# Gated products of an attention-and-GLU kernel: four pieces of 576 tokens, each as two halves of 288, in place of five pieces of up to 480

## The chip, the cores and the metric

The kernel runs on one core of one Trainium2 chip. The metric is the device time of one launch in microseconds (us); lower is better. The kernel before took 980.77 us (median of three runs, 980.37 to 981.58).

Five engines work side by side, each through its own queue in order: PE (TensorE; PEld is its weight load), DVE (VectorE), ACT (ScalarE), POOL (GpSimd) and SP (SyncE, which here issues every DMA). Engines wait for one another through semaphores.

## The reference

Queries are averaged in pairs (1152 to 576 rows per head), attention runs over 4 batches x 8 heads, and its result, 2304 tokens of 512 features, goes through a gated linear unit with a hidden width of 1536:

```python
q_pool = q.reshape(B, H, S // 2, 2, D).mean(axis=3)        # B=4, H=8, S=1152, D=64
scores = scale * np.matmul(q_pool, k.transpose(0, 1, 3, 2))
attn = softmax(scores)
x = np.matmul(attn, v)  ->  (2304, 512)
gate = 1.0 / (1.0 + np.exp(-(x @ w_gate)))                  # w_gate, w_val: 512 x 1536
out  = (gate * (x @ w_val)) @ w_out                         # w_out: 1536 x 512
```

## The kernel before, in words

Every float32 operand of a product is split into a high and a low fp32r part; a product of two operands is three matmuls (high x high, high x low, low x high).

**Attention.** Heads are taken one after the other (`attend`), each in two groups of 288 query columns (`GR`, `half`). Per head PE does the maxima's products (L354, 384 columns, reduced by DVE at L358), the scores (L438, two matmuls of 288), and the products with the values (L480 with the high part, L484 with the low part; in batch 0 L455). ACT takes the exponentials (L442, L470), DVE forms the low parts (L473), POOL sums the denominators (L502). Two heads make a pair; `normalise` divides the pair's result per group of 288 and writes the x tile's two parts: ACT the high (L594), POOL the low (L598).

**The gated part** (`gated`) runs per piece of tokens. A piece needs x of all four pairs of a batch. It has three thirds (`th`). A third makes four g tiles: each needs a gate and a value product of 12 matmuls over the piece's N tokens (`product`, L674), then tanh on ACT (L709), gate times value on DVE (L716), the split of g on ACT (L720) and POOL (L724). Then four output products (12 matmuls each, over the four g tiles), summed into `opart` by ACT (L749) or DVE (L751), and stored in the last third (L761). The weights are loaded by SP from a DRAM copy (L685): a wg tile (1 MB, gate and value) per g tile, a wo tile (0.5 MB) per output product; there are two wo slots. That DRAM copy is made by `convert` during the first batches: per tile two DVE instructions (L626, L631), three on ACT, one on POOL.

**Order.** The kernel hands every operation to a planner (`Plan`) with an engine, an assumed duration and a priority, and the planner writes out one fixed order per engine. `product` takes one of six PSUM banks (slot "b") and keeps it until ACT or DVE has read the result. The gated products of a piece get priorities spread over one batch's length, so that they lie between the attention of the next batch.

**Pieces.** `CUTS` (L167) divides the 2304 tokens at 480, 960, 1440 and 1920. A piece that crosses a batch's end waits for the next batch (L788 to 791), so one piece each follows batches 0, 1 and 2, and the last two pieces (480 and 384 tokens) follow batch 3, after all attention.

Of the kernel before, what the change touches and what calls it, by code (L numbers as in the profile page):

```python
# [158 lines left out]
def attention_glu_kernel(ctx: ExitStack, tc: tile.TileContext, qT, kT, vt_in, v, wg, wv, wo, out):  # L159
# [6 lines left out]
    CHUNK = 480  # L166
    CUTS = [min(k * CHUNK, B * SQ) for k in range(6)]  # L167
    NCH = len(CUTS) - 1

# [23 lines left out]
    LATE = {"x": 3, "wg": 1}  # L193
# [13 lines left out]
    def change_first():  # L207
# [13 lines left out]
    SHAPE = {"x": [128, 2, CHUNK], "wg": [128, 2, 2, 4, 128], "el": [128, GN], "acc": [128, GN],  # L221
# [25 lines left out]
        "g": tiles("g", [128, 2, CHUNK], F32R),  # L247
        "opart": tiles("opart", [128, CHUNK], F32),
# [4 lines left out]
        "sg": tiles("sg", [128, CHUNK], F32),  # L253
# [303 lines left out]
    def normalise(p, g, st):  # L557
# [23 lines left out]
        q = a  # L581
        while q < b:
            t = p // 4 * SQ + q
            c = max(k for k in range(NCH) if CUTS[k] <= t)
            o = t - CUTS[c]
            n = min(CUTS[c + 1] - t, b - q)
            key = (c, p % 4)
            first = key not in xs
            if first:
                xs[key] = (pl.hold("x"), [])  # L590
            xh, ops = xs[key]

            def hi(xh=xh, o=o, q=q, n=n):
                nc.scalar.activation(out=tl(xh)[:, 0, o:o + n], in_=tl(st["y"])[:, q:q + n], func=ACTF.Copy)  # L594

            def lo(xh=xh, o=o, q=q, n=n):
                x = tl(xh)
                nc.gpsimd.tensor_tensor(out=x[:, 1, o:o + n], in0=tl(st["y"])[:, q:q + n],  # L598
                                        in1=x[:, 0, o:o + n].bitcast(F32), op=ALU.subtract)

            f = pl.op("ACT", act(n), hi, s + 0.2, after=[nm], uses=[st["y"]] + ([] if first else [xh]),
                      take=[xh] if first else [])
            ops.append(pl.op("POOL", pool(n), lo, s + 0.2, after=[f], uses=[xh, st["y"]]))
            q += n

# [51 lines left out]
    def gated(ch, base, steps):  # L657
        base += 10
        step = steps / 36.0
        t0 = CUTS[ch]  # L660
        N = CUTS[ch + 1] - t0
        n_g = [0]
        acc = {}

        def product(at, parts, uses, after):
# [25 lines left out]
        for th in range(3):  # L691
            gs = {}
            for m_ in range(4 * th, 4 * th + 4):
                wh, lw = weights("wg", m_, base + step * n_g[0])
                sg, gh = pl.hold("sg"), pl.hold("g")
                for s in range(2):
                    at = base + step * n_g[0]
                    n_g[0] += 1

                    def parts(kc, wh=wh, s=s):  # L700
                        w, x = tl(wh), tl(xs[ch, kc][0])
                        return [(w[:, h, s, kc], x[:, l, 0:N]) for h, l in ((0, 0), (0, 1), (1, 0))]

                    ms, last = product(at, parts, lambda kc, wh=wh: [wh, xs[ch, kc][0]],
                                       lambda kc, lw=lw: [lw] + xs[ch, kc][1])
                    if s == 0:

                        def post(ms=ms, sg=sg):
# [22 lines left out]
            for dm in range(4):  # L731
# [3 lines left out]
                if th == 0:  # L735
                    acc[dm] = [pl.hold("opart"), None]
# [29 lines left out]
    xs = {}  # L766
# [80 lines left out]
```

## Time and profile before

| | us |
|---|---|
| median of three runs | 980.77 |
| the profiled execution | 980.11 |
| its span (all engines, first to last instruction) | 978.3 |
| PE / DVE / ACT / POOL busy | 935.5 / 697.7 / 636.0 / 682.1 |

The profile is one execution. Its page gives busy time by engine, a row of digits that shows each engine's busy share in 40 slices of 24.5 us, and the costliest groups of instructions with the mean duration of one. Matmuls overlap in PE's pipeline: one instruction is drawn some 300 to 380 ns long, though the next starts earlier. What a matmul costs is the distance between starts, and that is read from the timeline. "Idle before" an instruction is the time in which its engine did nothing, with the operation whose end released it.

### The profile page before, as it was taken

To read this page: it belongs to the slowest core of one execution; us is meant where nothing else is said; L and a number is where in the kernel's file an instruction comes from. 1 tells how busy PE (TensorE), PEld (TensorE's weight loads), DVE (VectorE), ACT (ScalarE), POOL (GpSimd) and SP (SyncE) were. 2 spreads that over 40 slices of the span, in tenths; PEclk is the share of its full clock that TensorE was granted. 3 is DMA by queue.
4 is the path that set the end of the run, shared out by engine and by line. 5 is a ranking of instruction groups with operands and counts; after the bars stand their busy time and mean duration, and the time that the engine had idled before them with its cause. 6 is when DMAs were issued, how large, how long until landed. Compare 5 with 4: busy or idle time off the path is not lost.

```text
span 978.3 us, 15851 instructions
## 1 busy us (share of the span) xinstructions
PE 935.5 (96%) x5136; PEld 837.3 (86%) x5136; DVE 697.7 (71%) x1386; ACT 636.0 (65%) x1605; POOL 682.1 (70%) x691
## 2 busy tenths in 40 slices
PE   6999999999879999999999999999999999999997
PEld 3878787988779888899889999998989888888996
DVE  6598888898988988887988898888988540111011
ACT  3779898978879668877776877777777632211211
POOL 7578797999998978888786887878877531211111
PEclk9999999999989999999999999999999999999999
DMA  7588887366876664345454455454342255656762
GB/s 169 150 263 257 274 267 232 118 216 201 258 263 198 214 216 144 102 136 156 133 154 140 134 157 154 137 163 147 105 131 87 86 187 198 215 189 242 255 248 86
DMA packets 54163, 175.62 MB, mean 180 GB/s; under 512 B 14656, under 2 KB 17216, under 8 KB 46400
## 3 DMA queue, kind: packets, MB, share of 16 engines
q1 hardware_dynamic: 54080, 174.61, 56.2%
q8 instruction: 40, 0.66, 0.3%
q14 instruction: 43, 0.35, 0.1%
HBM read 150.99 MB, written 23.59 MB: 178 GB/s over the span
## 4 chain that ended last, share of the span: by engine, by line
PE 77%; DVE 13%; ACT 5%; issue 2%; DMA 2%; POOL 1%; POOLq 0%; SPq 0%; ACTq 0%; DVEq 0%
PE bank L674 41%; PE bank L438 13%; PE bank L354 7%; PE bank L484 5%; PE bank L480 5%; PE bank L455 4%; DVE pm L358 3%; DVE cr L626 2%; DVE cr L631 2%; DMA wo<-wo_d 2%; DVE el L473 1%; DVE dh L545 1%; PE bank L487 1%; PE bank L549 1%; ACT eh L442 1%
## 5 line engine op out<-in xcount | busy, mean ns | idle before, releaser
L674 PE MATMUL bank<-x,wg 128*128 128x480 f32 (+1 forms) x1440 | 339.4, 373 | 0.9 <-ACT r L534 0.4
L358 DVE TENSOR_REDUCE pm<-bank 128x1 f32<-128x384 f32 x480 | 256.8, 549 | 46.0 <-PE bank L354 42.1
L674 PEld LDWEIGHTS bank<-x,wg 128*128 128x128 f32 x1440 | 259.5, 189 | 25.6 <-ACT r L534 1.6
L502 POOL TENSOR_TENSOR acc<-acc,eh 128x288 f32<-128x288 f32 x240 | 198.1, 825 | 59.4 <-ACT eh L442 48.6
L442 ACT ACTIVATE eh<-bank 128x288 fp32r<-128x288 f32 x432 | 176.6, 409 | 84.8 <-PE bank L438 79.6
L473 DVE TENSOR_TENSOR el<-bank,eh 128x288 fp32r<-128x288 f32 x432 | 192.2, 452 | 44.0 <-ACT bank L470 39.9
L354 PE MATMUL bank<-KA,QA 128*128 128x384 f32 x480 | 171.0, 372 | 12.1 <-ACT KA L336 7.9
L438 PE MATMUL bank<-QA,KA 128*128 128x288 f32 x576 | 173.4, 305 | 7.3 <-DVE sg L716 4.7
L470 ACT ACTIVATE bank<-bank 128x288 f32<-128x288 f32 x432 | 177.5, 411 | 0.0
L724 POOL TENSOR_TENSOR g<-sg,g 128x480 fp32r<-128x480 f32 (+1 forms) x60 | 71.3, 1189 | 143.3 <-ACT g L720 142.5
L674 PE MATMUL bank<-g,wo 128*128 128x480 f32 (+1 forms) x720 | 167.0, 371 | 4.3 <-DMA wo<-wo_d 2.1
L438 PE MATMUL bank<-QB,KB 128*128 128x288 f32 x576 | 169.3, 297 | 1.2 <-DVE QB L373 1.2
L674 PEld LDWEIGHTS bank<-g,wo 128*128 128x128 f32 x720 | 129.5, 188 | 19.0 <-DMA wo<-wo_d 3.1
L484 PE MATMUL bank<-el,vt 128*128 128x288 f32 x432 | 131.1, 304 | 7.0 <-DVE el L473 6.7
L480 PE MATMUL bank<-eh,vt 128*128 128x288 f32 x432 | 128.6, 298 | 2.1 <-ACT eh L442 2.1
L438 PEld LDWEIGHTS bank<-QA,KA 128*128 128x128 f32 x576 | 109.3, 190 | 16.7 <-DVE sg L716 5.0
L716 DVE SCALAR_TENSOR_TENSOR sg<-sg,bank 128x480 f32<-128x480 f32 (+1 forms) x60 | 37.8, 631 | 112.4 <-PE bank L674 111.6
L354 PEld LDWEIGHTS bank<-KA,QA 128*128 128x128 f32 x480 | 92.6, 194 | 28.5 <-DVE pm L358 13.9
L438 PEld LDWEIGHTS bank<-QB,KB 128*128 128x128 f32 x576 | 109.4, 190 | 3.3 <-DVE QB L373 1.7
L339 POOL TENSOR_TENSOR KB<-kr,KA 64x576 fp32r<-64x576 f32 x64 | 95.9, 1503 | 6.6 <-ACT KA L336 2.0
L484 PEld LDWEIGHTS bank<-el,vt 128*128 128x128 f32 x432 | 81.8, 189 | 16.8 <-DVE el L473 11.9
L720 ACT ACTIVATE g<-sg 128x480 fp32r<-128x480 f32 (+1 forms) x60 | 35.1, 585 | 88.8 <-DVE sg L716 67.7
(58 smaller groups left out, 1228.7 us busy)
## 6 DMA issues: line engine op xcount, KB each, us to landing
wg<-wg_d SPq DMA_DIRECT2D x60, 1024.0 KB, 4.9
wo<-wo_d SPq DMA_DIRECT2D x60, 512.0 KB, 3.7
kr<-in_kT_dram SPq DMA_DIRECT2D x64, 288.0 KB, 5.4
wg_d<-cs SPq DMA_DIRECT2D x24, 512.0 KB, 5.3
qr<-in_qT_dram SPq DMA_DIRECT2D x32, 288.0 KB, 4.3
vr<-in_v_dram SPq DMA_DIRECT2D x24, 288.0 KB, 4.2
cr<-in_wg_dram SPq DMA_DIRECT2D x12, 512.0 KB, 5.8
cr<-in_wv_dram SPq DMA_DIRECT2D x12, 512.0 KB, 4.8
```

Source lines behind the costliest of these rows:

```text
L339: nc.gpsimd.tensor_tensor(out=tl(kh)[1][HI, s], in0=tl(kr)[HI, s], in1=tl(kh)[0][HI, s].bitcast(F32), op=ALU.subtract)
L354: nc.tensor.matmul(out=tl(m)[:, 0:384], lhsT=tl(qh)[0][:, t * 128:(t + 1) * 128], rhs=tl(kh)[0][:, j * 384:(j + 1) * 384], start=True, sto ...
L358: nc.vector.tensor_reduce(out=tl(pm)[:, t, j:j + 1], in_=tl(m)[:, 0:384], axis=AXX, op=ALU.max)
L438: nc.tensor.matmul(out=tl(m)[:, 0:GN], lhsT=tl(hd["k"])[k][:, ks], rhs=tl(hd["q"])[k][:, a:b], start=(k == 0), stop=(k == 1))
L442: nc.scalar.activation(out=tl(eh), in_=tl(m)[:, 0:GN], func=ACTF.Exp, scale=1.0 / 16.0)
L470: nc.scalar.activation(out=p, in_=p, func=ACTF.Exp, scale=1.0 / 16.0)
L473: nc.vector.tensor_tensor(out=tl(el), in0=tl(m)[:, 0:GN], in1=tl(eh).bitcast(F32), op=ALU.subtract)
L480: nc.tensor.matmul(out=tl(av[0])[:, 0:GN], lhsT=pair(c, w), rhs=tl(eh), start=(c == 0), stop=(c == NC - 1))
L484: nc.tensor.matmul(out=tl(av[1])[:, 0:GN], lhsT=pair(c, 1 - w), rhs=tl(el), start=(c == 0), stop=(c == NC - 1 and not mine_c))
L502: nc.gpsimd.tensor_tensor(out=tl(acc), in0=tl(e0).bitcast(F32) if two else tl(acc), in1=tl(e1).bitcast(F32), op=ALU.add)
L674: nc.tensor.matmul(out=ps[:, 0:N], lhsT=l, rhs=r, start=(n == 0 and j == 0), stop=(n == 3 and j == 2))
L724: nc.gpsimd.tensor_tensor(out=g[:, 1, 0:N], in0=tl(sg)[:, 0:N], in1=g[:, 0, 0:N].bitcast(F32), op=ALU.subtract)
```

## The change

The pieces become the four batches, 576 tokens each. One weight tile brought in by DMA serves a whole piece, but no PSUM bank holds 576 float32 columns, so every product is made twice, for tokens 0 to 288 and 288 to 576 (`GR`), each half in a bank of its own with its own tanh, gate, split and output sum. The x tiles become 576 wide (8 in place of 12), the g and opart tiles 576 wide (4 each as before), the sg tiles 288 wide (4 in place of 2). `normalise` writes each group of 288 in one piece. Line numbers of the changed kernel: gated products L662, gate times value L706, weight loads L673, scores L434, value products L476 and L480, maxima L350 and L354, conversion L611 and L616.

```diff
-    CHUNK = 480
-    CUTS = [min(k * CHUNK, B * SQ) for k in range(6)]
-    NCH = len(CUTS) - 1
...
-        "y": 2, "r": 2, "tt": 1, "x": 12, "g": 4, "opart": 4, "wg": 3, "wo": 2, "cr": 3, "cs": 2, "sg": 2,
+        "y": 2, "r": 2, "tt": 1, "x": 8, "g": 4, "opart": 4, "wg": 3, "wo": 2, "cr": 3, "cs": 2, "sg": 4,
...
-    LATE = {"x": 3, "wg": 1}
+    LATE = {"x": 2, "wg": 1}
...
-        step = steps / 36.0
-        t0 = CUTS[ch]
-        N = CUTS[ch + 1] - t0
+        step = steps / 72.0
+        t0 = ch * SQ
...
-                        nc.tensor.matmul(out=ps[:, 0:N], lhsT=l, rhs=r, start=(n == 0 and j == 0), stop=(n == 3 and j == 2))
+                        nc.tensor.matmul(out=ps[:, 0:GN], lhsT=l, rhs=r, start=(n == 0 and j == 0), stop=(n == 3 and j == 2))
...
                 for s in range(2):
+                    for hf, (a, b) in enumerate(GR):
+                        at = now()
+                        if s == 0:
+                            sgs[hf] = [pl.hold("sg"), None]
+                        sg = sgs[hf][0]
+
+                        def parts(kc, wh=wh, s=s, a=a, b=b):
+                            w, x = tl(wh), tl(xs[4 * ch + kc, 0])
+                            return [(w[:, h, s, kc], x[:, l, a:b]) for h, l in ((0, 0), (0, 1), (1, 0))]
...
+            for dm in range(4):
+                wh, lw = weights("wo", 4 * th + dm, base + step * n_g[0])
...
+                for hf, (a, b) in enumerate(GR):
+                    at = now()
...
-        for ch in range(NCH):
-
-            if (CUTS[ch + 1] - 1) // SQ == b:
-                gated(ch, PB * (ch + 1), PB)
+        gated(b, PB * (b + 1), PB)
```

The planner writes a new order. Two places of it, before and after, follow. In the rows, `el`, `eh` are the parts of the exponentials, `vt` the values, `cr` the conversion's tile, `KA`/`QA`, `QB` the keys and queries; "waits" names the semaphore of the engine or DMA queue waited for.

The first place is in batch 1, some 285 us into the profiled execution, on DVE: two conversions follow each other. Before:

```order
L358 TENSOR_REDUCE pm_107<-bank 128x1 [waits PE_49]
L626 SCALAR_TENSOR_TENSOR cr_134<-cr_134 128x512 [waits DMAHW6_49]
L631 SCALAR_TENSOR_TENSOR cr_134<-cr_134 128x512 [waits DVE_49]
L626 SCALAR_TENSOR_TENSOR cr_135<-cr_135 128x512 [waits DMAHW3_49,Activation_49]
L631 SCALAR_TENSOR_TENSOR cr_135<-cr_135 128x512 [waits DVE_49]
L716 SCALAR_TENSOR_TENSOR sg_139<-sg_139,bank 128x480 [waits PE_49]
L473 TENSOR_TENSOR el_1426<-bank,eh_97 128x288 [waits Activation_49]
```

After:

```order
L354 TENSOR_REDUCE pm_107<-bank 128x1 [waits PE_49]
L611 SCALAR_TENSOR_TENSOR cr_131<-cr_131 128x512 [waits DMAHW6_49]
L616 SCALAR_TENSOR_TENSOR cr_131<-cr_131 128x512 [waits DVE_49]
L611 SCALAR_TENSOR_TENSOR cr_132<-cr_132 128x512 [waits DMAHW3_49]
L616 SCALAR_TENSOR_TENSOR cr_132<-cr_132 128x512 [waits DVE_49]
L706 SCALAR_TENSOR_TENSOR sg_136<-sg_136,bank 128x288 [waits PE_49]
L469 TENSOR_TENSOR el_1419<-bank,eh_97 128x288 [waits Activation_49]
```

Nothing moved on DVE: the four conversion instructions still stand together, with the gate product (now 288 wide) right behind them. PE at the same place, before:

```order
L484 MATMUL bank<-el_1425,vt_88 128x288 [waits DVE_49]
L438 MATMUL bank<-QA_79,KA_73 128x288
L438 MATMUL bank<-QB_82,KB_76 128x288
L480 MATMUL bank<-eh_97,vt_88 128x288 [waits Activation_49]
L354 MATMUL bank<-KA_74,QA_80 128x384 [waits DVE_49]
L438 MATMUL bank<-QA_79,KA_73 128x288 [waits DVE_49]
```

After:

```order
L480 MATMUL bank<-el_1418,vt_88 128x288 [waits DVE_49]
L434 MATMUL bank<-QA_79,KA_73 128x288
L434 MATMUL bank<-QB_82,KB_76 128x288
L350 MATMUL bank<-KA_74,QA_80 128x384 [waits DVE_49]
L476 MATMUL bank<-eh_97,vt_88 128x288 [waits Activation_49]
L662 MATMUL bank<-x_113,wg_127 128x288 [waits DVE_49]
```

In both the last row waits for DVE's gate product behind the conversions to give back its PSUM bank; a score's product stood there before, a gated product stands there now.

The second place is PE's end of the program: the last output products, over the four g tiles and alternating between the two wo slots. Before:

```order
L674 MATMUL bank<-g_122,wo_132 128x384 [waits DMAHW6_49]
L674 MATMUL bank<-g_122,wo_132 128x384 x2
L674 MATMUL bank<-g_123,wo_132 128x384 x3
L674 MATMUL bank<-g_124,wo_132 128x384 x3
L674 MATMUL bank<-g_125,wo_132 128x384 x3
L674 MATMUL bank<-g_122,wo_133 128x384 [waits DMAHW0_49,DVE_49]
```

After:

```order
L662 MATMUL bank<-g_119,wo_129 128x288 [waits DMAHW7_49,DVE_49]
L662 MATMUL bank<-g_119,wo_129 128x288 x2
L662 MATMUL bank<-g_120,wo_129 128x288 x3
L662 MATMUL bank<-g_121,wo_129 128x288 x3
L662 MATMUL bank<-g_122,wo_129 128x288 x3
L662 MATMUL bank<-g_119,wo_129 128x288 [waits DVE_49]
L662 MATMUL bank<-g_119,wo_129 128x288 x2
L662 MATMUL bank<-g_120,wo_129 128x288 x3
L662 MATMUL bank<-g_121,wo_129 128x288 x3
L662 MATMUL bank<-g_122,wo_129 128x288 x3
L662 MATMUL bank<-g_119,wo_130 128x288 [waits DMAHW2_49,DVE_49]
```

A wo tile now has 24 matmuls behind its one DMA wait, where it had 12. Over the whole program PE has 3456 gated matmuls of 288 columns where it had 1728 of 480 and 432 of 384. Behind the last attention matmul stand 909 gated matmuls of 288 now, and 453 of 480 and 432 of 384 before.

## Rows read from the trace of the kernel before

**Rows 1.** The page: span, busy time by engine, share, instructions.

```profile
span 978.3 us, 15851 instructions
PE 935.5 (96%) x5136; PEld 837.3 (86%) x5136; DVE 697.7 (71%) x1386; ACT 636.0 (65%) x1605; POOL 682.1 (70%) x691
```

**Rows 2.** Five stretches: length, busy by engine, granted clock, DMA share, GB/s.

```profile
240.00:300.00 60.00, 51.95 (x279) 47.12 (x280) 54.37 (x104) 49.49 (x120) 55.86 (x53) 0.91 0.73 237
300.00:400.00 100.00, 98.15 (x566) 88.60 (x565) 90.29 (x186) 75.32 (x199) 89.04 (x92) 1.00 0.54 180
400.00:794.00 394.00, 387.96 (x2274) 355.69 (x2273) 328.68 (x694) 290.11 (x773) 313.37 (x342) 1.00 0.44 136
...
0.00:794.00 794.00, 759.06 (x4252) 677.38 (x4253) 670.52 (x1340) 604.59 (x1547) 653.68 (x665) 0.99 0.56 174
794.00:978.30 184.30, 176.47 (x886) 159.94 (x884) 27.18 (x46) 31.44 (x58) 28.41 (x26) 1.00 0.59 205
```

**Rows 3.** PE's timeline, pieces of 480 and 384: start, length, line, operands, count.

```profile
829.92 5.37 PE L674 MATMUL bank<-g,wo 128*128 128x480 f32 x24
835.13 6.12 PE L674 MATMUL bank<-x,wg 128*128 128x480 f32 x27
...
940.37 4.38 PE L674 MATMUL bank<-g,wo 128*128 128x384 f32 x24
944.58 1.74 PE L674 MATMUL bank<-x,wg 128*128 128x384 f32 x9
```

**Rows 4.** The same view, first and last of two unbroken series of 288-column matmuls.

```profile
787.90 0.30 PE L484 MATMUL bank<-el,vt 128*128 128x288 f32 x1
...
789.10 0.38 PE L674 MATMUL bank<-g,wo 128*128 128x480 f32 x1
...
468.86 0.29 PE L484 MATMUL bank<-el,vt 128*128 128x288 f32 x1
...
470.05 0.34 PE L354 MATMUL bank<-KA,QA 128*128 128x384 f32 x1
```

**Rows 5.** Groups by form: busy us, mean ns of one, idle before and releasers.

```profile
L473 DVE TENSOR_TENSOR el<-bank,eh 128x288 fp32r<-128x288 f32 x432 | 192.2, 452 | 44.0 <-ACT bank L470 39.9
L438 PEld LDWEIGHTS bank<-QA,KA 128*128 128x128 f32 x576 | 109.3, 190 | 16.7 <-DVE sg L716 5.0 <-ACT e L442 3.0 <-DVE el L473 1.1
L716 DVE SCALAR_TENSOR_TENSOR sg<-sg,bank 128x480 f32<-128x480 f32 x48 | 31.2, 650 | 66.6 <-PE bank L674 65.8
L598 POOL TENSOR_TENSOR x<-y,x 128x288 fp32r<-128x288 f32 x20 | 16.6, 831 | 3.3 <-ACT x L594 3.0
```

**Rows 6.** PE's waits and DVE's conversions near 254 and 287 us, timelines.

```profile
254.67 0.61 PE L484 MATMUL bank<-el,vt 128*128 128x288 f32 x1 [2.26 <-DVE el L473]
...
286.69 0.61 PE L438 MATMUL bank<-QA,KA 128*128 128x288 f32 x1 [4.71 <-DVE sg L716]
...
281.34 1.06 DVE L626 SCALAR_TENSOR_TENSOR cr<-cr 128x512 uint32<-128x512 uint32 x1
...
286.00 0.64 DVE L716 SCALAR_TENSOR_TENSOR sg<-sg,bank 128x480 f32<-128x480 f32 x1
```

**Rows 7.** Short stretches behind those waits, columns as in the five stretches.

```profile
256.00:258.00 2.00, 2.00 (x7) 1.82 (x7) 1.66 (x4) 1.86 (x5) 2.00 (x2) 0.51 0.43 145
...
290.00:292.00 2.00, 2.00 (x8) 1.79 (x7) 0.92 (x3) 0.00 (x0) 2.00 (x3) 0.50 0.96 348
```

**Rows 8.** PE's timeline where attention ends, and at the program's end.

```profile
793.94 2.11 PE L674 MATMUL bank<-g,wo 128*128 128x480 f32 x9
...
965.07 2.72 PE L674 MATMUL bank<-g,wo 128*128 128x384 f32 x14 [0.66 <-POOL g L724]
969.42 2.37 PE L674 MATMUL bank<-g,wo 128*128 128x384 f32 x12 [1.63 <-DMA wo<-wo_d]
972.42 2.33 PE L674 MATMUL bank<-g,wo 128*128 128x384 f32 x12 [0.63 <-DVE opart L751]
```

**Rows 9.** SP's DMA issues of the last two wo tiles.

```profile
965.71 0.32 SPq L685 DMA_DIRECT2D wo<-wo_d  x1
...
967.82 0.32 SPq L685 DMA_DIRECT2D wo<-wo_d  x1
```

More of the change, by code (lines that the diff above doesn't have):

```diff
@@ L580, in normalise, with hi, lo @@
             nm = pl.op("POOL", pool(GN), mult, s, after=[nm], uses=[st["y"], st["r"]])
[L581 to L604, printed above, removed]
+        if (p, 0) not in xs:
+            xs[p, 0] = xs[p, 1] = pl.hold("x")
+        xh = xs[p, g]
+        def hi():
+            nc.scalar.activation(out=tl(xh)[:, 0, a:b], in_=tl(st["y"])[:, a:b], func=ACTF.Copy)
+        def lo():
+            x = tl(xh)
+            nc.gpsimd.tensor_tensor(out=x[:, 1, a:b], in0=tl(st["y"])[:, a:b], in1=x[:, 0, a:b].bitcast(F32),
+                                    op=ALU.subtract)
+        f = pl.op("ACT", act(GN), hi, s + 0.2, after=[nm], uses=[st["y"]] + ([xh] if g else []), take=[] if g else [xh])
+        x_done[p, g] = pl.op("POOL", pool(GN), lo, s + 0.2, after=[f], uses=[xh, st["y"]])
     def convert(kind, m, s, due):
@@ L694, in gated @@
                 wh, lw = weights("wg", m_, base + step * n_g[0])
[L695 removed]
+                gh, sgs, ga = pl.hold("g"), {}, []
                 for s in range(2):
[L697 to L708, printed above, removed]
[L709 to L730 removed]
@@ L731, in gated @@
-            for dm in range(4):
-                at = base + step * n_g[0]
-                n_g[0] += 1
-                wh, lw = weights("wo", 4 * th + dm, at)
-                if th == 0:
-                    acc[dm] = [pl.hold("opart"), None]
-                oh, prev = acc[dm]
-                def parts(i, wh=wh, gs=gs):
-                    w, g = tl(wh), tl(gs[i][0])
-                    return [(w[:, h, 0, i], g[:, l, 0:N]) for h, l in ((0, 0), (0, 1), (1, 0))]
-                ms, last = product(at, parts, lambda i, wh=wh, gs=gs: [wh, gs[i][0]], lambda i, lw=lw, gs=gs: [lw, gs[i][1]])
-                def post(ms=ms, oh=oh, th=th):
-                    o, ps = tl(oh)[:, 0:N], tl(ms)[:, 0:N]
-                    if th == 0:
-                        nc.scalar.activation(out=o, in_=ps, func=ACTF.Copy, scale=0.5)
-                    else:
-                        nc.vector.scalar_tensor_tensor(out=o, in0=ps, scalar=0.5, in1=o, op0=ALU.mult, op1=ALU.add)
-                if th == 0:
-                    a = pl.op("ACT", act(N), post, at - 1, after=[last], uses=[ms], take=[oh])
-                else:
-                    a = pl.op("DVE", dve(N), post, at - 1, after=[last, prev], uses=[ms, oh])
-                acc[dm][1] = a
-                if th == 2:
-                    def store(dm=dm, oh=oh):
-                        nc.sync.dma_start(out=out[dm * 128:(dm + 1) * 128, t0:t0 + N], in_=tl(oh)[:, 0:N])
-                    pl.op("SP", dma(N / 2), store, at, after=[a], uses=[oh], late=3.0)
```

75 lines of the change are left out of this document (53 added, 22 removed).

## The prediction

> **What bounds the kernel now.** I read the page's busy line first: PE is busy 935.5 of 978.3 us, no other engine over 71% [rows 1]. Then the stretches: from 400 to 794 us PE is idle only 394 - 387.96 = 6.0 us, and from 794 us to the end it works almost alone, with DVE, ACT and POOL at 27 to 31 us of 184 [rows 2]. So the time is PE's instruction stream from end to end, plus its gaps. The attention is done at about 794 us, and what follows is the rest of the gated part. Only between 240 and 300 us does PE lose much: 8 us of idle and a granted clock of 0.91 [rows 2]. There DVE runs conversions back to back (281.34 to 286.00), PE waits 2.26 and 4.71 us [rows 6], and after each wait the clock is at its lower level, 0.5 of full speed (1.2 instead of 2.4 GHz), for some us [rows 7].
>
> With PE the bound, what I need is a matmul's price. The drawn length is not it; the distance of starts is. 24 matmuls of 480 columns take 835.13 - 829.92 = 5.21 us, 0.2171 each; 24 of 384 columns 944.58 - 940.37 = 4.21 us, 0.1754 each [rows 3]. Nine of 288 columns, each with another stationary operand, take 789.10 - 787.90 = 1.20 us, 0.1333 each; in another such series of nine 470.05 - 468.86 = 1.19, 0.1322 each [rows 4].
>
> **The change part by part.**
>
> *Gated matmuls.* Before: 1728 x 0.2171 + 432 x 0.1754 = 375.1 + 75.8 = 450.9 us. After: 3456 x 0.1333 = 460.7 us. The columns are the same; what grows is the number of matmuls, by 1296, and with it the part of a matmul that does not shrink with its width. **+9.8 us**, all of it on the path. Bounds: with the faster series (0.1322) 456.9, +6.0; with the line through the two wider shapes, which puts 288 columns at 0.1754 - 0.0417 = 0.1337, 462.1, +11.2. I take 0.1333, which lies between.
>
> 288 columns at the full 2.4 GHz alone are 0.120 us, so the rows show some 0.013 us per matmul beside the columns [rows 4]. The Trainium skill ("TensorE: Matmul & The Clock Gate", "Wait — 56ns, not 53.3ns?") gives a warm start-to-start of N / 2.4 GHz plus about 2.5 ns. By that estimate the pieces would be 420.1 us before and 423.4 after, and this term +3.3. The trace disagrees: 0.1333 where the page has 0.1225, and the row decides.
>
> The loads into the array stay one per matmul (the order still alternates stationary operands), so 1296 are added. They are hidden: 190 ns long, beside matmuls that start every 0.133 us [rows 4, 5]. The "one weight load" is the DMA's: 12 fewer of 1 MB and 12 fewer of 0.5 MB, all beside PE work except at the program's end.
>
> *Work behind the products.* Halves cost DVE 0.452 us each (nearest row, another 288-wide read of PSUM) where 480 tokens cost 0.650, and POOL 0.831 each [rows 5]. Over the program that is some 9 us more for DVE and POOL each. Cover: these engines are idle for over 150 us of the end [rows 2], and before it they gain time. Of the gated columns 2547 of 3456 (74%) now lie beside attention, up from 1275 x 480 / 995,328 (61%); PE's stretch to 794 us grows by 2547 x 0.1333 - 1275 x 0.2171 = 339.5 - 276.8 = 62.7 us. DVE, at 670.5 of 794 (84%) there [rows 2], gets about 14 us more (74% of 160 halves at 0.452, less 61% of the 63 us that its gated work takes now), so 685 of 857 (80%); POOL goes from 82% to about 77%. So I do not expect more gaps from load, and count **-1.0 us** of the 6.0 in the long stretch. Bounds: -7 (of the 7.9 us of idle from 300 to 794 us almost all goes) and +8 (below). If the cover were gone, 9 us of DVE would be on the path.
>
> *The two stops at 254 and 287 us.* DVE's order there is unchanged, and PE's last row before the stop still waits for the gate product behind four conversion instructions. **0.** If they go, it is a rival.
>
> *The end.* From the last attention matmul, PE takes 793.94 to 972.42 + 2.33 = 974.75, 180.8 us [rows 8]. Its matmuls are 453 x 0.2171 + 432 x 0.1754 = 174.1, so 6.7 us are lost, for the most part before output products: with two wo slots a wo tile's load can start only when the tile two before it is used up. The last two are issued at 965.71 and 967.82 and used at 969.42 and 972.42, 3.7 and 4.6 us later [rows 8, 9] (the wait named DVE is the second load: DVE's sum is not an input of that product). In between lies one product of 12 x 0.1754 = 2.1 us. After the change a wo tile holds 24 x 0.1333 = 3.2 us, so a late tile costs 0.5 to 0.8 us, with one such pair in each of three thirds (six thirds before): some 3 us in all. The last g tile's halves are ready earlier too, which ends the 0.66 us wait. **-3.7 us**; between -6.7 (no waits) and +1 (a wait at each of twelve tiles, 0.65 each, on 6.7). Behind the last matmul stand DVE's sum and a store, 3.55 us now, with less to write: **-0.2**.
>
> Sum on the profiled execution: 980.1 + 9.8 - 1.0 - 3.7 - 0.2 = 985.0 us. The median of the runs is 0.7 above that execution, so 985.5 as a round number for a median.
>
> **The rivals.**
>
> *A, the stops go (faster).* At the halves' finer grain PE finds work while DVE converts, and both stops with their slow stretches fall away: 2.26 + 4.71 us of wait, and about 8.6 us at half speed, 254.67 to 258 and 286.69 to 292, of which half is lost [rows 6, 7]: 11.3 us in all, 974.2. Against it: the order, in which the same wait stands in both. It decides if PE has 4 us of ready matmuls between the conversions' start and that wait; the order has six instructions there.
>
> *B, the gaps of the steady part go (no change, or a little faster).* Shares of 80% in place of 84% let PE run without a break after 300 us: 6.9 us below the forecast, 978.6; with half of it, 982. For it: the shares. Against: idle there is 2% already, and it comes from single late results, not from load.
>
> *B2, a narrower fixed cost.* At 0.1322 a matmul the term is +6.0, and the time 981.7; the faster series of rows 4 speaks for it, the other against. By the fixed cost that the Trainium skill gives (the page and section above) the time would be 979.0, which neither series bears out.
>
> *C, less work per bank (slower still).* Six banks hold PE's lead over DVE and ACT. A half product is 12 x 0.1333 = 1.6 us of PE work in a bank where 480 columns were 2.6, so at each late DVE or ACT result PE can run dry 1.0 us earlier. It decides where a result is late by more than the banks hold, which is where PE is idle now: 7.9 us from 300 to 794 us [rows 2]. If those gaps double, the time is 993.4. The busy shares speak against it.
>
> *D, the array's loads set the pace.* If a matmul could start only every 190 ns, the length of a load [rows 5], 3456 would take 656.6 us and the time be near 1190. Rows 4 show loads and matmuls at 0.133, which all but excludes it. The Trainium skill ("TensorE: Matmul & The Clock Gate", "Back-to-back issue gap") says that the spacing is set by both load and matmul; the trace shows the matmul alone setting it at this width.
>
> **How the numbers follow.** Forecast 0.48, A 0.12, B 0.15, B2 0.10, C 0.14, D 0.01. A change of under 0.2% (978.8 to 982.7) can't be told from none by a measurement of this kernel. Faster: A, a third of B, and 0.02 for gains from elsewhere, 0.19. Same: the rest of B, B2, and the lower edge of the forecast, 0.20. Slower: 0.61. The range, 976 to 992, leaves out A and the far end of C and takes in all bounds of the first term; the forecast's own range is 982 to 989.
>
> **What would show it.** The 288-column matmuls of L662 should start 0.133 us apart in the last 120 us, and PE's last attention matmul should end near 856 us. The tail from there to PE's last matmul should be near 124 us, with waits for wo under 1 us each. The stop of over 4 us behind the conversions should still be there, with a granted clock of 0.5 after it. The forecast is wrong if the distance is under 0.130, if the attention ends before 850 or after 862 us, or if that stop is gone.

## The result, and the profile after

The changed kernel takes 964.22 us (median of four runs, 962.17 to 965.67) against 980.57 (four runs, 980.06 to 981.58): ratio 0.983, 95% interval 0.9811 to 0.985. Slower was forecast, 985.5, with a range of 976 to 992; it is 16 us faster. The profiled execution took 965.67 us, 14.4 less than the one before, and its span shrinks by as much.

The page of the changed kernel (span; busy time by engine):

```profile
span 963.9 us, 18546 instructions
PE 930.3 (97%) x6432; PEld 895.0 (93%) x6432; DVE 705.5 (73%) x1446; ACT 654.2 (68%) x1677; POOL 682.2 (71%) x715
```

Its stretches, with the columns of [rows 2]; of the last two, one ends and the other begins where attention ends:

```profile
240.00:300.00 60.00, 52.21 (x362) 50.31 (x361) 50.12 (x97) 48.91 (x122) 56.16 (x53) 0.97 0.69 211
...
300.00:400.00 100.00, 98.87 (x718) 97.29 (x717) 87.83 (x183) 76.39 (x198) 88.84 (x92) 1.00 0.59 187
...
0.00:835.70 835.70, 808.23 (x5521) 774.05 (x5522) 683.54 (x1398) 629.57 (x1619) 661.26 (x689) 1.00 0.53 166
835.70:963.90 128.20, 122.02 (x913) 120.96 (x911) 21.98 (x49) 24.65 (x58) 20.96 (x26) 1.00 0.42 143
```

PE's timeline after the change, where attention ends and in the tail (start, length, line, operands, count, idle before):

```profile
835.71 0.43 PE L545 MATMUL bank<-dh,sel 128*128 128x288 f32 x2
835.97 2.95 PE L662 MATMUL bank<-g,wo 128*128 128x288 f32 x21
...
879.88 3.42 PE L662 MATMUL bank<-g,wo 128*128 128x288 f32 x24 [1.38 <-DMA wo<-wo_d]
883.14 25.27 PE L662 MATMUL bank<-x,wg 128*128 128x288 f32 x189
908.24 6.52 PE L662 MATMUL bank<-g,wo 128*128 128x288 f32 x48
...
953.20 6.70 PE L662 MATMUL bank<-g,wo 128*128 128x288 f32 x48 [0.59 <-DVE opart L742]
```

The distance of the new matmuls is (908.24 - 883.14) / 189 = 0.1328 us. The tail runs from 835.97 to 953.20 + 6.70 = 959.90, 123.9 us, as forecast. But attention ends at 836 and not near 856.

The stop behind the conversions is still there. PE's waits after the change, which answer to [rows 6]:

```profile
251.14 0.66 PE L662 MATMUL bank<-x,wg 128*128 128x288 f32 x3 [1.07 <-DVE y L527]
...
273.11 0.40 PE L434 MATMUL bank<-QB,KB 128*128 128x288 f32 x1 [1.78 <-POOL QB L369]
...
292.72 1.57 PE L662 MATMUL bank<-x,wg 128*128 128x288 f32 x5 [4.32 <-DVE sg L706]
```

DVE's timeline ahead of the last of them, and four stretches of the same kernel: one behind each of the first two waits, the one behind the stop, and the next:

```profile
286.88 1.21 DVE L611 SCALAR_TENSOR_TENSOR cr<-cr 128x512 uint32<-128x512 uint32 x1
...
290.53 1.77 DVE L616 SCALAR_TENSOR_TENSOR cr<-cr 128x512 uint32<-128x512 uint32 x1
292.23 0.44 DVE L706 SCALAR_TENSOR_TENSOR sg<-sg,bank 128x288 f32<-128x288 f32 x1
```

```profile
254.00:256.00 2.00, 2.00 (x17) 2.00 (x16) 1.62 (x4) 2.00 (x6) 1.84 (x3) 1.00 0.57 140
...
274.00:276.00 2.00, 2.00 (x17) 2.00 (x16) 1.09 (x3) 0.87 (x3) 1.97 (x2) 1.00 0.64 143
...
294.00:296.00 2.00, 2.00 (x11) 2.00 (x10) 1.25 (x3) 0.90 (x3) 1.49 (x2) 0.57 0.68 252
296.00:298.00 2.00, 2.00 (x16) 2.00 (x15) 1.34 (x4) 1.89 (x5) 1.59 (x2) 1.00 1.09 309
```

Four conversions, then the gate product, then PE after 4.32 us (4.71 before), then a granted clock of 0.57 (most of that stretch at the lower level, 0.5): much as forecast, though the slow stretch is over at 296 us, some 3 us after the wait (at least 5 before [rows 6, 7]). The other slow stretch, near 256 us [rows 7], is gone.

**Where the time came from.** PE is the bound in both, so the account is its own. Each matmul has a usual distance to the next start (0.1328 us at 288 columns, 0.1754 at 384, 0.2171 at 480; [rows 3] and above). What its distance has beyond that I call loss; time at the lower clock counts in it too. Drawn idle doesn't show all of it. PE's timeline of the kernel before:

```profile
465.83 0.29 PE L438 MATMUL bank<-QA,KA 128*128 128x288 f32 x1
465.96 0.29 PE L438 MATMUL bank<-QB,KB 128*128 128x288 f32 x1
466.09 0.34 PE L354 MATMUL bank<-KA,QA 128*128 128x384 f32 x1
466.56 0.93 PE L674 MATMUL bank<-x,wg 128*128 128x480 f32 x3
467.32 0.29 PE L484 MATMUL bank<-el,vt 128*128 128x288 f32 x1
```

From 466.09 to 466.56 are 0.47 us where 0.175 is usual: 0.29 lost, and no bracket, since a matmul is drawn longer than its distance. I summed the loss over three stretches of attention, cut at the same attention matmul in every kernel (the 790th and the 1550th of 2976, give or take one) and named by the batch they mostly hold: batch 0, batch 1, and batches 2 and 3. The stretches of batch 1 and of batches 2 and 3, first before, then after:

```profile
179.40:403.80 224.40, 212.09 (x1197) 191.34 (x1197) 201.62 (x400) 177.70 (x452) 206.53 (x205) 0.98 0.62 203
403.80:793.00 389.20, 383.16 (x2246) 351.24 (x2245) 325.25 (x685) 286.96 (x764) 309.81 (x338) 1.00 0.44 135
```

```profile
182.40:417.00 234.60, 225.03 (x1616) 220.76 (x1616) 203.50 (x420) 185.62 (x476) 212.13 (x215) 0.99 0.62 196
417.00:834.10 417.10, 417.02 (x3071) 416.12 (x3070) 333.45 (x722) 303.25 (x816) 313.22 (x356) 1.00 0.40 126
```

Batch 1: 224.4 us, of which 106.0 are attention's matmuls, 94.4 gated ones and 24.0 loss; after, 234.6 with 113.5 gated and 15.2 loss. Batches 2 and 3: 389.2 with 198.2 attention, 177.8 gated and 13.2 loss (drawn idle shows 6.0 of it); after, 417.1 with 218.3 gated and 0.6 loss. These sums hold to about 1 us.

The 13.2 us are not all of one kind. Of what is drawn as idle in batches 2 and 3 of the kernel before, most is one wait, three times over (us in total, times, longest):

```profile
PE bank L549 <- DVE dh L545: 3.9, 3, 1.8
```

`dh` is the denominators' tile, an input of L549 and no bank. By distances these three waits are 4.4 of the 13.2 us; the changed kernel has none of them there.

### The profile page after: what moved, and what is told of

It is laid out like the page before. It is cut to its first block, busy times and chain, and to the rows that moved or that the text cites. A ratio compares the mean times of both kernels' runs of the same rounds, so it can differ in the third digit from the quotient of the medians.

```text
span 963.9 us, 18546 instructions
## 1 busy us (share of the span) xinstructions
PE 930.3 (97%) x6432; PEld 895.0 (93%) x6432; DVE 705.5 (73%) x1446; ACT 654.2 (68%) x1677; POOL 682.2 (71%) x715
## 4 chain that ended last, share of the span: by engine, by line
PE 70%; DVE 2%; POOL 2%; ACT 2%; DMA 1%; issue 1%; ACTq 0%; POOLq 0%
PE bank L662 42%; PE bank L434 10%; PE bank L350 5%; PE bank L476 5%; PE bank L480 5%; PE bank L545 1%; PE bank L483 1%; POOL acc L498 1%; DMA cr<-in_wv_dram 1%; DMA wo<-wo_d 1%; DVE cr L616 0%; POOL QB L369 0%; ACT bank L466 0%; ACT eh L438 0%; DVE cr L611 0%
## 5 line engine op out<-in xcount | busy, mean ns | idle before, releaser
L662 PE MATMUL bank<-x,wg 128*128 128x288 f32 x2304 | 357.7, 296 | 5.8 <-DVE sg L706 4.3
L662 PEld LDWEIGHTS bank<-x,wg 128*128 128x128 f32 x2304 | 332.5, 188 | 7.4 <-DVE sg L706 4.6
L354 DVE TENSOR_REDUCE pm<-bank 128x1 f32<-128x384 f32 x480 | 258.5, 551 | 60.5 <-PE bank L350 54.2
L350 PE MATMUL bank<-KA,QA 128*128 128x384 f32 x480 | 171.8, 370 | 13.7 <-ACT KA L332 8.1
L662 PE MATMUL bank<-g,wo 128*128 128x288 f32 x1152 | 177.0, 295 | 2.6 <-DMA wo<-wo_d 1.4
L434 PE MATMUL bank<-QA,KA 128*128 128x288 f32 x576 | 172.8, 303 | 2.7 <-ACT e L438 1.2
L434 PE MATMUL bank<-QB,KB 128*128 128x288 f32 x576 | 169.1, 297 | 2.9 <-POOL QB L369 1.8
L662 PEld LDWEIGHTS bank<-g,wo 128*128 128x128 f32 x1152 | 164.9, 188 | 3.7 <-ACT opart L740 1.6
L714 POOL TENSOR_TENSOR g<-sg,g 128x288 fp32r<-128x288 f32 x96 | 79.7, 830 | 117.4 <-ACT g L710 115.9
L476 PE MATMUL bank<-eh,vt 128*128 128x288 f32 x432 | 128.1, 297 | 0.9 <-ACT eh L438 0.8
L480 PE MATMUL bank<-el,vt 128*128 128x288 f32 x432 | 128.0, 296 | 0.3 <-DVE el L469 0.2
L350 PEld LDWEIGHTS bank<-KA,QA 128*128 128x128 f32 x480 | 92.4, 193 | 27.9 <-DVE pm L354 15.2
L434 PEld LDWEIGHTS bank<-QA,KA 128*128 128x128 f32 x576 | 109.4, 190 | 6.4 <-ACT e L438 1.8
L434 PEld LDWEIGHTS bank<-QB,KB 128*128 128x128 f32 x576 | 109.3, 190 | 4.0 <-POOL QB L369 2.0
L706 DVE SCALAR_TENSOR_TENSOR sg<-sg,bank 128x288 f32<-128x288 f32 x96 | 43.2, 450 | 86.8 <-PE bank L662 84.6
L335 POOL TENSOR_TENSOR KB<-kr,KA 64x576 fp32r<-64x576 f32 x64 | 91.7, 1439 | 6.1 <-ACT KA L332 2.0
L476 PEld LDWEIGHTS bank<-eh,vt 128*128 128x128 f32 x432 | 81.1, 188 | 1.6 <-ACT eh L438 1.6
L480 PEld LDWEIGHTS bank<-el,vt 128*128 128x128 f32 x432 | 81.4, 188 | 1.3 <-DVE el L469 1.2
```

The lines of the kernel that those rows point to most:

```text
L335: nc.gpsimd.tensor_tensor(out=tl(kh)[1][HI, s], in0=tl(kr)[HI, s], in1=tl(kh)[0][HI, s].bitcast(F32), op=ALU.subtract)
L350: nc.tensor.matmul(out=tl(m)[:, 0:384], lhsT=tl(qh)[0][:, t * 128:(t + 1) * 128], rhs=tl(kh)[0][:, j * 384:(j + 1) * 384], start=True, sto ...
L354: nc.vector.tensor_reduce(out=tl(pm)[:, t, j:j + 1], in_=tl(m)[:, 0:384], axis=AXX, op=ALU.max)
L434: nc.tensor.matmul(out=tl(m)[:, 0:GN], lhsT=tl(hd["k"])[k][:, ks], rhs=tl(hd["q"])[k][:, a:b], start=(k == 0), stop=(k == 1))
L476: nc.tensor.matmul(out=tl(av[0])[:, 0:GN], lhsT=pair(c, w), rhs=tl(eh), start=(c == 0), stop=(c == NC - 1))
L480: nc.tensor.matmul(out=tl(av[1])[:, 0:GN], lhsT=pair(c, 1 - w), rhs=tl(el), start=(c == 0), stop=(c == NC - 1 and not mine_c))
```

## The experiments

"Before" ran beside each job, with medians from 977.8 to 979.6 us. Gated work and loss in us, worked out as above:

| run | us | ratio, 95% interval | batch 1: gated, loss | batches 2, 3: gated, loss |
|---|---|---|---|---|
| before | 980.57 | 1 | 94.4, 24.0 | 177.8, 13.2 |
| after | 964.22 | 0.9811 to 0.985 | 113.5, 15.2 | 218.3, 0.6 |
| e1_five_halved | 1004.46 | 1.025 to 1.0299 | 97.3, 29.0 | 185.3, 1.7 |
| e2_384_192 | 993.31 | 1.0132 to 1.0188 | 124, 9.7 | 236, 0.6 |
| e3_spread_1_2 | 983.31 | 1.003 to 1.007 | 97.2, 27.0 | 217.2, 7.6 |
| e4_g_split_whole | 971.86 | 0.9916 to 0.9963 | 113.6, 17.7 | 218.3, 6.5 |
| e5_posts_halved | 983.04 | 1.0039 to 1.0076 | 93.1, 27.6 | 179.2, 13.1 |
| e6_pieces_472 | 985.05 | 1.0042 to 1.008 | 92.2, 31.4 | 176.2, 12.6 |
| e7_sg_two | 963.61 | 0.9835 to 0.9875 | 113.5, 14.0 | 218.3, 0.6 |
| e8_rest_spread_1_2 | 967.01 | 0.9874 to 0.9903 | 113.1, 15.6 | 201.3, 5.2 |
| e9_before_fourteen | 1039.20 | 1.0609 to 1.0647 | 109.4, 15.9 | 208.6, 8.1 |
| e10_after_two_of_three | 870.01 | 0.8849 to 0.8922 | 74.6, 42.0 | 146.1, 27.7 |
| e11_after_units_of_six | 963.73 | 0.9838 to 0.9869 | 114, 17.6 | 218.3, 1.4 |
| e12_before_single_units | 987.92 | 1.0076 to 1.0131 | 95.3, 34.0 | 177.4, 11.6 |
| e13_after_ten_of_twelve | 907.47 | 0.9242 to 0.9301 | 94.0, 29.8 | 181.9, 6.4 |
| e14_halves_in_turn | 986.25 | 1.0046 to 1.0106 | 114.7, 22.8 | 219.5, 15.6 |
| e15_all_posts_halved | 985.56 | 1.0039 to 1.0077 | 93.8, 32.1 | 179.1, 10.7 |
| e16_after_base_0 | 957.69 | 0.975 to 0.9799 | 114.7, 12.8 | 217.9, 1.5 |
| e17_after_five_banks | 977.17 | 0.996 to 0.9987 | 110.4, 19.1 | 218.3, 12.2 |

Two theories. The *amount*: the other engines set how long a stage of attention takes, and the more gated work stands beside it, the less PE waits. The *halves*: something in the narrower pieces of work keeps PE fed. The expectations call the first the share and the second the grain, and their steady stages are batches 2 and 3 in three equal parts.

**Halves without the four pieces, and other widths.** e1 keeps the five pieces and halves each product; e2 has the four pieces, cut unevenly.

```diff
+        N = (CUTS[ch + 1] - t0) // 2
+        HV = ((0, N), (N, 2 * N))
```

> The five pieces of before (480, 480, 480, 480, 384), each product in two halves (240 or 192 columns). The share of gated columns beside attention stays at 61%. By the line through the measured distances (0.1328 at 288, 0.1754 at 384, 0.2171 at 480) a 240-column matmul costs 0.112 us and a 192-column one 0.091: 3456 x 0.112 + 864 x 0.091 = 466 us, 15 more than before. Theory grain (a gated product that holds PE, its bank and the engines behind it for a shorter time lets PE run without gaps): PE idle in the long stretch from some 400 us to the end of attention falls from 6.0 us to under 1, and 13 to 19 us of lost time go, so 975 to 983 in all. Theory share (more gated work beside each head leaves the other engines time): idle there stays near 6 us, and the time is near 995.

```diff
+    GG = ((0, 384), (384, 576))
...
-                    for hf, (a, b) in enumerate(GR):
+                    for hf, (a, b) in enumerate(GG):
```

> Four pieces of 576 as in the changed kernel, cut 384 + 192 in place of 288 + 288. Same share beside attention (74%), same PE work (0.1754 + 0.091 = 0.266 per pair, as 2 x 0.1328), coarser grain (a product of 2.1 us and one of 1.1 where both were 1.6). Theory share: PE idle in the long stretch stays under 1 us and the time within 3 us of the changed kernel's 964. Theory grain: half of the gaps come back, idle 2 to 4 us there, and the time is 968 to 975.

Both are slower than before and than either theory had them, because of a price: 192 columns were expected to cost 0.091 us. PE's timeline of e1, 240 and 192 columns:

```profile
892.12 5.58 PE L679 MATMUL bank<-g,wo 128*128 128x240 f32 x48
897.53 1.48 PE L679 MATMUL bank<-x,wg 128*128 128x192 f32 x12
...
904.75 20.25 PE L679 MATMUL bank<-x,wg 128*128 128x192 f32 x180
924.83 5.41 PE L679 MATMUL bank<-g,wo 128*128 128x192 f32 x47
```

(897.53 - 892.12) / 48 = 0.1127 and (924.83 - 904.75) / 180 = 0.1116 us: 192 columns cost as much as 240. So e1's gated work is 1728 x 2 x 0.1127 + 432 x 2 x 0.1116 = 485.9 us, 35 more than before, while the time rose by 27 over the kernel before in the same job (977.76). In batches 2 and 3 it loses 1.7 us in place of 13.2 with only 7.5 us more gated work; in batch 1 nothing is won. The amount alone doesn't explain the first, the halves alone not the second. e2 keeps the changed kernel's small loss in batches 2 and 3 (0.6 us) with uneven halves, but has 18 us more gated work there, so it doesn't tell the two apart.

**The order of the pieces.**

```diff
-        gated(b, PB * (b + 1), PB)
+        gated(b, PB * (b + 1), PB * 1.2)
```

> The changed kernel with the priorities of a piece's gated products spread over 1.2 batch lengths in place of one, so that 2412 of 3456 (70%, from 74%) gated matmuls stand before the last attention matmul; the halves stay. Theory grain: no gaps in the long stretch (idle under 1 us); the attention ends some 18 us earlier and the tail is 18 us longer, 964 to 967 in all. Theory share: a third of the way back to the share of before (61%) brings back a third of the lost time or more, idle 2 to 4 us in the long stretch, 970 to 978 in all.

```diff
+        gated(b, PB * (b + 1), PB * (1.0 if b == 0 else 1.2))
```

> The changed kernel with the priorities of the pieces of batches 1 to 3 (not the first) spread over 1.2 batches. In the run with all four spread, gated work beside batch 1 fell from 113.6 to 97.2 us, the loss there rose from 15.2 to 27.0, and the three steady stages lost 7.6 in place of 0.6. Theory of the share: with the first piece left where it is, batch 1 keeps 110 to 114 us of gated work and 14 to 17 us of loss, and only the steady part's 7 us come back: 968 to 973. If both come from the spread itself wherever it stands, the time goes to 979 to 985 again.

e3 missed both ranges: one number in the priorities undoes the whole gain (983.31). Batch 1 has 16 us less gated work and loses 12 us more. With the first piece left alone (e8, 1 us under its range), batch 1 is back at 113.1 and 15.6; over both stretches 5.0 us more are lost than in the changed kernel, where e3 lost 18.8 more.

**What order alone does**, by pieces of 472 tokens (CHUNK = 472 in the kernel before):

> The kernel before with pieces of 472 tokens instead of 480 (the last one 416): work on TensorE the same by its distances (450.9 us), the instructions per piece as many, other order in places. A control for what the planner's choice of order alone does: 976 to 984 if the order by itself is worth no more than about 4 us, and 13 us of loss in the three steady stages again. Below 970 the comparison of before and after would rest on a chance of the order and not on halves of 288. By the theory of the share it loses slightly more in batch 1 (the four pieces beside attention hold 369.1 us in place of 375.1), +0 to +2.

A miss by 1 us: 985.05. The loss in batches 2 and 3 is that of before, but batch 1 loses 31.4. Over the eight kernels with 92 to 97 us of gated work beside batch 1 its loss is 24.0 to 34.0, and before has the lowest. These kernels differ in more than their order; e6, which changes little else, has 7.4 us more than before. So several us of a batch-1 loss can hang on the planner's order, and before may have drawn well.

**Width and grain.** e4 splits g once, 576 wide, on ACT and POOL; e5 halves tanh, gate and split of the five pieces; e15 the sums of the output too; e7 has two sg buffers.

```diff
+                            if hf:
+                                o = pl.op("ACT", act(SQ), hi, at - 1, after=td, uses=[sg], take=[gh])
+                                ga.append(pl.op("POOL", pool(SQ), lo, at - 1, after=[o], uses=[sg, gh]))
```

> The changed kernel with the split of a g tile done once for 576 tokens on ACT (some 0.67 us in place of 2 x 0.44) and POOL (some 1.44 us in place of 2 x 0.83); products, tanh and gate stay in halves. Share stays 74%, PE's grain stays, only the grain of ACT and POOL is coarse, even coarser than before (0.60 and 1.23 us). Less work on ACT and POOL. Theory share: idle in the long stretch stays under 1 us, 962 to 966. Theory grain, in the form that long POOL and ACT instructions make attention's results late: idle 2 to 5 us there, 968 to 975.

```diff
+        HV = ((0, N // 2), (N // 2, N))
...
+                        for hf, (a, b) in enumerate(HV):
...
+                            def post(ms=ms, sg=sg, a=a, b=b):
+                                nc.scalar.activation(out=tl(sg)[:, a:b], in_=tl(ms)[:, a:b], func=ACTF.Tanh, scale=0.5)
```

> The kernel before, its five pieces and its products of up to 480 columns unchanged; only what is done with each product of the first half of the computation is cut in two: tanh, gate, and the two parts of the split run over 240 columns twice (192 in the last piece) on ScalarE, VectorE and GpSimd. TensorE's gated work stays at 450.9 us. Theory of the grain (in the three steady stages of attention, 404 to 793 us, the 13.2 us that TensorE's starts stand further apart than its pitches come from 480-wide instructions on the other engines, behind which small ones that release a bank stand): these 13.2 us fall to 2 to 4, and the time to 968 to 973. Theory of the share (TensorE loses less because more of its own work stands beside attention, which is not so here): 13.2 stays at 10 to 15, and the time stays at 976 to 984, or above by what the added instructions cost. Both: batch 1's loss of 24.0 us stays at 20 to 28, since VectorE and GpSimd have no less to do there.

> The kernel before with everything behind its products in halves of 240, the additions to the output parts too, the products on TensorE whole. In the run with tanh, gate and split halved the steady stages still lost 13.1 us. If the 480-wide additions to the output (0.65 us each on VectorE) were what was left of the grain, the loss there falls to 0 to 4: 968 to 974. If the width of these instructions doesn't matter: 10 to 15 again, 980 to 986.

```diff
-        "cr": 3, "cs": 2, "sg": 4,
+        "cr": 3, "cs": 2, "sg": 2,
```

> The changed kernel with two buffers for the gate (sg) in place of four, all else as it is: the halves stay, the buffers that let one half be worked on while the next three are filled do not. If the four buffers carry the gain in the steady stages, the 0.6 us of loss there go back to 6 or more and the time to 970 to 976; if the narrow instructions carry it, the time stays at 962 to 967.

Narrow instructions on the other engines alone bring little or nothing (13.1 and 10.7 us where 13.2 were; both kernels are slower than before), and the four sg buffers nothing. The whole split of e4 costs 6 us in batches 2 and 3; which of its waits does it was not separated.

PE's unit, six matmuls in the changed kernel, one in the kernel before:

```diff
-            for n in range(4):
+            for u in range(2):
...
-                last = pl.op("PE", 3 * pe(GN), mm, at + 0.05 * n, after=dep, uses=uses(n) + ([m] if n else []),
+                last = pl.op("PE", 6 * pe(GN), mm, at + 0.05 * (6 * u / 3), after=dep, uses=us + ([m] if u else []),
```

> The changed kernel with its gated matmuls placed on TensorE in units of six (0.80 us, which no attention matmul can enter) instead of three (0.40 us; before had three of 480 columns, 0.65 us). Work, other instructions and buffers are the same. If it is the shorter unit on TensorE that took the losses away, those of the steady stages go from 0.6 back to 10 or more and the time to 974 to 980. By the share: 0 to 2 there, 962 to 967.

> The kernel before with its gated matmuls placed on TensorE one at a time (0.217 us) instead of in threes (0.65 us): the other way round. If the unit on TensorE is what counts, the 13.2 us of loss in the steady stages fall to 0 to 4 and the time to 966 to 971; by the share they stay at 10 to 15 and the time at 976 to 984.

Neither does what the unit would: 1.4 and 11.6 us in batches 2 and 3. e12's time, 4 us above what was expected, comes from batch 1 (34.0).

**The amount.**

```diff
+            def twice():
+                for l, r in parts(0)[:2]:
+                    nc.tensor.matmul(out=tl(m)[:, 0:N], lhsT=l, rhs=r, start=True, stop=True)
+
+            last = pl.op("PE", 2 * pe(N), twice, at, after=[d for k in range(4) for d in after(k)], uses=uses(0), take=[m])
```

> The kernel before, with two of a product's matmuls issued twice (14 matmuls to a product for 12; the two extra ones are written over), all else as it was. TensorE's gated work becomes 450.9 x 14/12 = 526.0 us, 75.1 more, with the 480-wide instructions and units of before. Beside batch 1 there stand about 110 us of it (94.4 before, 113.6 in the changed kernel), in a steady stage of attention 68 (59 before, 73 changed). Theory of the share (what else stands on the other engines sets the length of a stage, and TensorE's losses are what its own work doesn't fill): the loss in batch 1 falls from 24.0 to 12 to 17, in the steady stages from 13.2 to 1 to 4, and the time rises by 54 to 59 only: 1032 to 1037. Theory of the grain (narrower pieces of work fill the gaps): losses stay, 1050 to 1057.

```diff
-                    for j, (l, r) in enumerate(parts(n)):
+                    for j, (l, r) in enumerate(parts(n)[:2]):
```

> The changed kernel with every third gated matmul left out (the product of the weights' low part with the inputs' high part, 8 matmuls to a product for 12): gated work 459.0 x 2/3 = 306.0 us, the halves of 288, their other instructions and their buffers as they are. Beside batch 1 some 76 us of it are left (113.6), in a steady stage 49 (73). Theory of the grain: the losses stay at 15.2 and 0.6 us and the time falls by the whole 153 us, to 808 to 815. Theory of the share: batch 1 keeps a length of 220 to 235 us and the steady stages one of 120 to 127 us (137 to 140 now), so that 25 to 40 us of loss appear in batch 1 and 20 to 45 in the steady stages: 855 to 890.

```diff
+                    for j, (l, r) in enumerate(parts(n)[:2 if n < 2 else 3]):
```

> The changed kernel with two of a product's twelve gated matmuls left out (the low part of the weights with the high part of the inputs, for the first two of four contraction chunks): gated work 459.0 x 10/12 = 382.5 us, so that beside attention about as much of it stands as in the kernel before (94.7 us beside batch 1 where before had 94.4, some 61 in a steady stage, 59 in before), but in halves of 288 columns. The time if no loss changes: 964 - 76.5 = 888. If the amount of TensorE's work alone sets the loss: back to about 24 in batch 1 and 13 in the steady stages, 906 to 911. If batch 1 follows the amount and the steady stages follow the halves: 24 and 1 to 4, 896 to 901. If only the halves count: 15 and 1, 886 to 890.

e10's stretches, batch 1 and batches 2 and 3:

```profile
183.00:405.60 222.60, 199.19 (x1324) 185.27 (x1323) 201.77 (x419) 183.26 (x476) 210.18 (x213) 0.98 0.62 203
405.60:777.60 372.00, 359.52 (x2527) 346.27 (x2526) 327.24 (x723) 301.53 (x816) 317.17 (x357) 1.00 0.44 141
```

153 us of matmuls are left out, and the time falls by 94 only. Batch 1 keeps 222.6 us (220 to 235 were expected), in which POOL is busy 210.18 and DVE 201.77, as much as before and after. From e10 to the changed kernel 38.9 us of gated work are added there and the batch grows by 12.0; in batches 2 and 3 72.2 are added and they grow by 45.1. From the other side, e9's 75.1 us of extra matmuls cost 61 us, 2 more than the amount alone was to cost: batch 1 did as expected (15.9), batches 2 and 3 did not (8.1 for 1 to 4). e13, halves at the amount of before, loses 29.8 us in batch 1, so the halves save nothing there; in batches 2 and 3 it loses 6.4, between the two theories. Its 907.5 us lies in the range of the amount alone by two misses that cancel: more loss in batch 1 than that theory had, less in the others. It is the sum: 964.2 - 76.5 + 14.6 + 5.8 = 908.1. None of the three is the amount alone: with the number of matmuls in a product, the time that it holds its bank changes too, by their matmuls 3.0 us in e9 (2.6 before), 1.1 in e10 and 1.3 in e13 (1.6 in the changed kernel). That doesn't explain these runs: the loss fell with the longer hold and rose with the shorter ones.

**What the halves do: banks.** e14 issues the two halves of a product in turn, so that both banks are held at once; e17 takes one bank of six away.

```diff
+            m, last, ends = [pl.hold("b") for _ in range(2)], None, []
             for n in range(4):
+                for hf in range(2):
```

> The changed kernel with the two halves of a product issued in turn, three matmuls of one and three of the other, instead of one half after the other: each of their two banks is then held about twice as long (24 matmuls from its first to its last instead of 12, so 3.1 us of matmuls instead of 1.6; a product of 480 before held one for 2.6). Work, instructions and widths are the same. If what the halves take away in the steady stages is the long hold of one of six banks, the loss there goes from 0.6 to 8 or more, and in batch 1 from 15 to 20 or more: 975 to 990. If the hold doesn't count: 962 to 968.

```diff
-        "b": 6, "n": 2, "K": 3, "Q": 3,
+        "b": 5, "n": 2, "K": 3, "Q": 3,
```

> The changed kernel with five PSUM banks for its products and attention in place of six, all else as it is. Holding both halves' banks at once (in turn) took one bank more on average while a product runs, and brought the loss in batch 1 from 15.2 to 22.9 us and in batches 2 and 3 from 0.6 to 15.6. If the cause there is the number of banks left, five banks do nearly the same: 8 or more in batches 2 and 3, 20 or more in batch 1, 975 to 990. If it is that two halves end together and send their tanh, gate and split at once, five banks change little: 0.6 to 4 there and 962 to 970.

Both come out as the banks would have it, but for batch 1 of e17 (19.1 where 20 or more was expected). The stretch of batches 2 and 3, first of e14, then of e17:

```profile
423.20:856.50 433.30, 430.68 (x3080) 418.05 (x3079) 327.26 (x723) 298.98 (x816) 316.00 (x355) 1.00 0.38 122
```

```profile
418.40:847.10 428.70, 425.82 (x3072) 416.73 (x3071) 326.77 (x721) 302.46 (x816) 313.90 (x356) 1.00 0.39 123
```

The same work takes 433.3 and 428.7 us in place of 417.1, and hardly any of it is idle on the page: the loss is in short stops. PE's timeline of e14 has one:

```profile
695.34 0.85 PE L350 MATMUL bank<-KA,QA 128*128 128x384 f32 x2
696.12 0.66 PE L662 MATMUL bank<-g,wo 128*128 128x288 f32 x3
```

0.78 us for two matmuls of 0.1754, no bracket: 0.43 lost. Five banks bring most of it back without issuing the halves in turn, so it doesn't take two halves that end together. What PE waited for in e17's stretch, the longest in total:

```profile
PE bank L662 <- ACT r L530: 1.3, 4, 0.5
```

`r` is no input of a gated product. L530 reads attention's result out of its bank, so these four waits are for a bank.

**A faster version.** With each piece due 10 us earlier:

```diff
-        base += 10
+        base += 0
```

> The changed kernel with its gated pieces due 10 us earlier each (base += 0 for 10), the candidate for a faster one: some more gated work reaches batch 1 (about 5 us more, worth 2 to 3 us of its 15.2 us of loss by the slope of the runs so far, 0.45 us per us), and as much less is left behind attention. By the share 960 to 963; if the start of a piece collides with the conversions, 966 to 972.

957.69 us, ratio 0.9774, below both kernels (its interval lies under that of after) and below both ranges that were expected. PE's timeline where its attention ends:

```profile
836.61 0.42 PE L545 MATMUL bank<-dh,sel 128*128 128x288 f32 x2
836.87 24.87 PE L662 MATMUL bank<-x,wg 128*128 128x288 f32 x186
```

Attention ends 0.9 us later than in the changed kernel, but with 852 gated matmuls left instead of 909, 7.6 us less. They went into batch 0 (11.6 us of gated work, 4.8 in after) where I had expected batch 1; the losses of batches 0 and 1 fell by 3.5 and 2.4 us.

## Why the prediction was wrong

- *Gated matmuls, +9.8:* 3456 x 0.1328 = 459.0 against 450.9, **+8.1**. Right, inside its bounds of 6.0 and 11.2.
- *Gaps in attention, -1.0 with bounds -7 and +8:* **the step that failed: -19.5.** Up to the last attention matmul PE takes 835.97 - 793.94 = 42.0 us more [rows 8]; gated work there grew from 450.9 - 174.1 = 276.8 to 459.0 - 909 x 0.1328 = 338.3, by 61.5. By stage: batch 1 -8.8, batches 2 and 3 -12.6, batch 0 about +2.
- *The two stops, 0:* one is much the same in place and size, with a shorter slow stretch; the other became 1.07 and 1.78 us without a slow stretch behind either. Both differences are part of batch 1's -8.8. Rival A (both go) did not happen.
- *The end, -3.7:* 123.9 us with 909 x 0.1328 = 120.7 of matmuls, 3.2 lost where 6.7 were, **-3.5**. Right; the longest wait for wo, 1.38, is over the 1 us forecast.
- *Store, -0.2:* 963.9 - 959.9 = 4.0 against 3.55, **+0.45**.

8.1 - 19.5 - 3.5 + 0.45 = -14.45; measured -14.4.

The failed step had three faults. First, it read the gaps from drawn idle: 7.9 us from 300 to 794 us, so that -7 was the most that could go. That the idle comes from single late results fits most of what is drawn (3.9 of 6.0 us wait for `dh`), but not the rest of the loss. By distances of starts 13.2 were lost there, and 24.0 in batch 1, whose loss the forecast put down to the two stops (11.3 us in rival A). Second, it said "I do not expect more gaps from load" from the shares 84% and 80%, and it counted the added PE work beside attention as all on the path. In batch 1 POOL is busy 92% and DVE 90% before, and e10 against the changed kernel shows there that of added PE work about a third lengthens the batch (12.0 of 38.9 us). Rival B, the gaps of the steady part, was the right place for 12.6 of the 19.5 us and had 0.15, but with 6.9 us as its price. Third, the only thought given to the banks, rival C, seems to have their sign wrong: it took a half product's shorter lead as a loss. Two banks at a time and five instead of six (e14, e17) show that the banks are short, and a half gives its bank back after 1.6 us of matmuls instead of 2.6. Rival D, which e1's distances exclude as well, was priced wrongly: 985.5 + 656.6 - 460.7 is 1181, not near 1190.

How the -19.5 divides: batch 1's -8.8 goes with the amount (e9 gets -8.1 with the old widths, e13 nothing with the new ones), though the planner's order alone moves that number by nearly as much (7.4 in e6), so how much of it is luck of the order stays open. In batches 2 and 3 the amount with the old widths gives -5.1 (e9), the halves at about the old amount -6.8 to -11.5 (e13, e1); together they leave 0.6, so the two overlap and can't be added. That the shorter hold of a bank is what the halves do there is inferred from e14 and e17, not shown by itself. A third of what went there, the 4.4 us of waits for `dh`, was no wait for a bank, and no run separates why those waits went: e5 has hardly any of them (0.2 us) and still loses 13.1.

## What to carry to other kernels

Where one engine is the bound and others are close behind it in a stage, work added to the bound engine in that stage is partly free, and work taken out of it saves only a part of its time: price it by that stage's length in two runs with different amounts, not by the program's shares. Take a pipelined engine's losses from the distances of its starts, not from the idle that is drawn. Count how long a unit of work holds a scarce buffer, and not only how much work it gives.

## What was not expected of the hardware

A matmul with its own weight load hardly got cheaper from 240 columns to 192: 0.1127 and 0.1116 us (e1), against 0.1328 at 288, 0.1754 at 384 and 0.2171 at 480. On the line through the two widest, 240 columns would be 0.1128 and 192 would be 0.0920, so 240 still lies on it and 192 doesn't. Rival D's pace (0.190, the drawn length of a load) is not reached, but between 240 and 192 columns something keeps the distance near 0.11; whether the loads set it no run here shows, and so the forecast's sentence that the matmul alone sets the pace fits 240 columns and more, not 192.
